# A recurrent attention with a gated layer behind it: the second sub of tokens also in fp16 pairs, and the lowest bits of a decoded weight written by ScalarE

## The chip, the core and the metric

The kernel runs on one NeuronCore of a Trainium2 chip. The metric is the device time of the core in microseconds, lower is better. Three runs of the kernel before gave 606.37, 607.78 and 608.83 us; the median is 607.78.

## What is computed

Cut to what matters:

```python
k_n = k / (norm(k) + 1e-6)                    # batch 4, 8 heads, 768 steps, 48 wide
for t in range(768):
    y[t] = q[t] @ state                       # read before the write
    v_old = k_n[t] @ state
    state = state + beta[t] * outer(k_n[t], v[t] - v_old)
x = y as 3072 tokens x 384
out = ((x @ w_a) * (x @ w_b)) @ w_out         # 384 -> 1536 -> 384
```

All of it is float32 at the interface. The weights reach the kernel as eight bytes per number (a double), and are turned into float32 on the chip.

## The kernel before, in words

**Attention.** The 768 steps are cut into 24 chunks of 32 steps, each with all 32 heads. For every chunk, TensorE makes the grams of k with k and of q with k (step G), VectorE solves a triangular system by 31 pairs of a multiplication and a subtraction (`solve`, tiles `tmp` and `b`), and then come the steps that hang on the state: K (`duo<-sh,rawb`, what the state gives), the subtraction `f`, U (`duo<-f,tt`), A (`duo<-u,at`, the output) and S (`S_ps<-u,knb`, the new state). Four chunks make a group, whose solve is one run on VectorE; `prep` makes its grams. In the first group the solve is by halves, which adds steps W and X (`bank<-b,tt`, `bank<-b,mk`, `bank<-wr,xn`). Chunks 0 and 1 run ahead of everything else.

**The gated layer.** Two chunks are a sub of 256 tokens; there are 12 subs. A sub is worked off in 12 units, one for each 128 of the 1536 inner columns (`moe`). A unit is `ab` (both products with w_a and w_b, into one PSUM bank), a copy `a` by ScalarE, the product `g` by VectorE, and two units later `moe_out`, the product with w_out that is summed over the 12 units in two banks. For the first `FULL` = 2 subs all of this is in float32: a unit is 6 matmuls of 128x256 for `ab` and 2 of 128x384 for the output, each of which the trace records twice. For the other ten, every operand is a pair of fp16 numbers, high and low part, and three of the four products are made: 18 matmuls for `ab` and 6 for the output. That asks for more on the other engines: `g` is cut into `ghl` (a cast by ScalarE, a subtraction by VectorE), a chunk's output is scaled and cut (four squares on ScalarE with `n`, a sum over partitions by TensorE, some ten short VectorE operations, `xb`), and the weights are cut into pairs.

**The weights.** `decode` makes float32 of a weight's 12 blocks, 1152 columns each, from the two words of a double: one shift (`TENSOR_SCALAR`), then two operations (`SCALAR_TENSOR_TENSOR`) that put in the sign and top bit and the lowest three bits; all three are VectorE's. Blocks lie in three staging slots (`late`, and two in `stage`), so block b + 3 is loaded only when block b is decoded; blocks 3 to 5 have places of their own in `wt`. `scales` squares each block (ScalarE, `sqw`), sums (TensorE), and when all 12 are there makes the scales: one matmul `norm,ones`, some dozen short VectorE operations from `sg` to `zw`, `gs` and `po`, then squares of w_out and a second matmul `so,ones`. `split` then writes high parts (ScalarE, `ACTIVATE wt<-wt,zw`) and low parts (VectorE, `SCALAR_TENSOR_TENSOR wt<-wt,zw` twice and `wt<-wt,eo` once a block).

**What sets the order.** Nearly every instruction is recorded by `Plan` and issued in an order that `pack` makes from a table of prices and of due times (`slot`, `when`, the `plan.due` lines); that is why the profile shows L560 for almost all. `merge`, `weave` and the calls at the end of `tile_kernel` set only the sequence in which work is recorded. Loads are chained by one-element copies on GpSimd so that few are under way at a time. Matmuls into `bank` use four PSUM banks shared by all; `duo` and `S_ps` have two each.

```python
V.tensor_scalar(d, hi, 5, 2, op0=ALU.logical_shift_left, op1=ALU.logical_shift_right)
V.scalar_tensor_tensor(d, hi, -0x40000000, d, op0=ALU.bitwise_and, op1=ALU.bitwise_or)
V.scalar_tensor_tensor(d, lo, 29, d, op0=ALU.logical_shift_right, op1=ALU.bitwise_or)
```

Of the kernel before, what the change touches and what calls it, by code (L numbers as in the profile page):

```python
# [30 lines left out]
NFC = FF // P  # L31

HALVES = [1, 0, 0, 0, 0, 0]
FULL = 2


LEADS = 4.0
BASE, FRESH, UNIT = 38e3, 4.6e3, 3.6e3


def when(v):
    n = NFC * FULL
    return BASE + (v * FRESH if v < n else n * FRESH + (v - n) * UNIT)


def finish(c):
    return 6 * c - 6 - (-2.5 if c == 4 else min(LEADS, 0.5 * max(0, c - 5)))


def slot(c, piece):  # L50
    if piece == "G" and c < 4:
        v = -30 + 0.1 * c
    elif c < 2:
        v = {
            0: {"W": -20, "X": -19, "U": -17, "A": -13.1, "S": 1.0},
            1: {"W": -15.2, "X": -14, "K": -15, "Q": -11.1, "U": -13, "A": -11, "S": 2.0},
        }[c].get(piece, -30)
    elif c < 4 and piece != "G":
        v = {
            2: {"W": 2.5, "X": 3.2, "K": 3.8, "U": 4.6, "S": 5.2, "A": 5.8},  # L60
            3: {"W": 6.2, "X": 6.8, "K": 7.4, "U": 8.2, "A": 9.0, "S": 10.4},
        }[c].get(piece, -30)
    elif piece == "G":
        v = 5.0 + 2.2 * (c - 4) if c < 8 else finish(c // 4 * 4 - 4 + c % 4 // 2) - 0.5 + 0.1 * (c % 2)
    else:
        v = finish(c) - {"W": 7, "X": 6.5, "K": 5.5, "U": 4.0, "S": 3, "A": 1.5}[piece]
    return when(v)


EARLY = [(0, "k"), (0, "b"), (2, "k"), (0, "r"), (2, "r")], [(0, "m"), (0, "v"), (2, "v"), (0, "w"), (1, "w")], [(2, "w")], [(3, "w"), (4, "w"), (4, "k"), (4, "r"), (5, "w")], [(6, "w"), (6, "k"), (6, "r"), (7, "w"), (4, "v"), (6, "v"), (8, "w")]  # L70
SHARE, QUOTA = {32: 0.24, 48: 0.19, 64: 0.5}, 1515.0
# [14 lines left out]
class Plan:  # L86
# [53 lines left out]
    def region(self, ap):  # L140
# [14 lines left out]
        p0, free = divmod(low, el)  # L155
        parts, mask = 1, (1 << (size // 2)) - 1
        for st, n in reversed([(abs(d[0]), d[1]) for d in ap.ap]):
# [171 lines left out]
    def pack(self, pri, back=False):  # L329
# [18 lines left out]
        while len(done) < n:  # L348
# [215 lines left out]
def tile_kernel(ctx, tc, kqt, kqs, kn, vn, beta, w, masks, picks, out):  # L564
# [162 lines left out]
    def scales():  # L727
        for b in range(NFC):
            v = wf[:, plain(b) : plain(b) + 6 * P]
            sq = sqr()  # L730
            plan.due = when(b + 8)
            plan.behind = set(hold)
# [15 lines left out]
            yield  # L748
        plan.due = when(15)
        t = att()  # L750
# [20 lines left out]
        V.tensor_scalar_mul(big[:, 3:4], big[:, 1:2], 2.0**-25)  # L771
        V.tensor_scalar_mul(eo, po, big[:, 2:3])
        yield

# [96 lines left out]
    def prep(g):  # L871
        chs = GROUPS[g]
        ss = sst
        for c in chs[::2]:
            kept = list(hold)
            hold.extend(opened[NFC + 1 : NFC + 2] if g == 2 else [])
            if g > 1:
# [244 lines left out]
    def steps(g, chs):  # L1122

        for c in chs:
# [290 lines left out]
    for c, what in EARLY[3]:  # L1415
        load(c, what)
    run_all(ws[3])
    queue.extend((s, list(range(NFC))) for s in range(2))
    load(0, "s")
    V.tensor_copy(sum16, sel[:, 0:P])  # L1420

    def weave(g, steps_):
# [128 lines left out]
```

## Time and profile before

| | |
|---|---|
| median of the three runs | 607.78 us |
| profiled execution, first to last instruction | 604.4 us |
| TensorE busy | 597.3 us (99%) |
| VectorE busy | 405.2 us (67%) |
| ScalarE busy | 300.6 us (50%) |
| granted TensorE clock | 1.00 in the whole span |

The profile gives the profiled execution's time as its span, and no other; the median stands 3.4 us above it, which is taken as what lies around the span. Times in the rows are counted from the start of the span. A row of the timeline has a start, a length, the engine, the line, the operation with the tile written and the tiles read, its shape and count, and in brackets how long the engine had been idle and what released it. A float32 matmul is two records, and so is a small one.

### The profile page before, as it was taken

How to read it: one execution, taken by the hardware profiler on the slowest of the kernel's cores; microseconds unless marked ns; L12 is line 12 of the kernel's file. 1: busy time of each engine (PE TensorE's matmuls, PEld its weight loads, DVE VectorE, ACT ScalarE, POOL GpSimd, SP SyncE). 2: the span in 40 equal slices, each digit the busy share in tenths (PEclk: the TensorE clock that was granted, in tenths of full speed). 3: DMA queues.
4: the chain of work that ended last, by engine and by line, in shares of the span. 5: the costliest groups of instructions: out<-in, count | busy, mean ns of one | idle time of the engine just before them, and what ended most of it. 6: DMA issues, size and time to landing. Idle time of an engine off the chain costs nothing.

```text
span 604.4 us, 25265 instructions
## 1 busy us (share of the span) xinstructions
PE 597.3 (99%) x11473; PEld 466.3 (77%) x11473; DVE 405.2 (67%) x1093; ACT 300.6 (50%) x756; POOL 34.9 (6%) x49
## 2 busy tenths in 40 slices
PE   8999999999999999999999999999999999999997
PEld 5487867777777778787878778778878878887875
DVE  5997888999799824898654996454995244244222
ACT  4321323698754664466455457545446535535332
POOL 1011320001100101000101001001000000000000
PEclk9999999999999999999999999999999999999999
DMA  5738681612212004103032021010000000000000
GB/s 207 288 123 312 243 309 36 210 71 87 73 58 98 29 29 150 38 30 124 3 89 95 3 91 61 4 54 3 3 28 4 2 28 2 3 29 2 27 1 26
DMA packets 11931, 46.46 MB, mean 77 GB/s; under 512 B 1328, under 2 KB 4784, under 8 KB 8752
## 3 DMA queue, kind: packets, MB, share of 16 engines
q1 hardware_dynamic: 11824, 44.85, 21.1%
q8 instruction: 89, 1.46, 1.0%
q14 instruction: 18, 0.15, 0.1%
HBM read 40.13 MB, written 4.72 MB: 74 GB/s over the span
## 4 chain that ended last, share of the span: by engine, by line
PE 82%; DVE 7%; DMA 5%; ACT 4%; issue 1%; POOL 0%; SPq 0%; POOLq 0%; DVEq 0%
PE bank L560 68%; PE duo L560 11%; DVE wt L560 4%; PE S_ps L560 3%; DMA rawb<-in_kqt 2%; ACT sqf L560 1%; DMA stage<-in_w 1%; DVE b L560 1%; ACT wt L560 1%; DMA late<-in_w 1%; DMA vnb<-in_vn 1%; DVE tmp L560 1%; PE bank L551 0%; ACT y L560 0%; DVE g L560 0%
## 5 line engine op out<-in xcount | busy, mean ns | idle before, releaser
L560 PE MATMUL bank<-xb,wt 128*128 128x256 f16 (+1 forms) x1800 | 246.9, 291 | 0.0
L560 PEld LDWEIGHTS <-wt 128*128 128x128 f16 x2160 | 208.2, 98 | 35.1 <-issue 0.2
L560 DVE TENSOR_TENSOR g<-bank,a 128x256 f32<-128x256 f32 x144 | 60.4, 419 | 117.2 <-ACT a L560 116.2
L560 PE MATMUL bank<-wt,ghl 128*128 128x384 f16 x720 | 136.7, 326 | 0.0
L560 ACT ACTIVATE a<-bank,gs 128x256 f32<-128x256 f32 x120 | 56.7, 472 | 125.1 <-PE bank L560 124.7
L560 PEld LDWEIGHTS <-ghl 128*128 128x128 f16 x720 | 67.5, 98 | 34.6
L560 PE MATMUL bank<-stage,wt 128*128 128x256 f16 x648 | 76.7, 273 | 0.0
L560 DVE TENSOR_TENSOR ghl<-g,ghl 128x256 f16<-128x256 f32 x120 | 51.3, 427 | 33.9 <-ACT ghl L560 33.3
L560 ACT CAST ghl<-g 128x256 f16<-128x256 f32 x120 | 48.4, 403 | 50.3 <-DVE g L560 50.1
L560 PEld LDWEIGHTS bank<-xb,wt 128*128 128x128 f32 x288 | 53.6, 190 | 10.7 <-DVE xb L560 0.5
L560 DVE TENSOR_TENSOR b<-b,tmp 128x31 f32<-128x31 f32 (+20 forms) x170 | 56.5, 332 | 3.6
L560 DVE TENSOR_TENSOR tmp<-b,b 128x31 f32<-128x31 f32 (+20 forms) x170 | 56.3, 331 | 3.6
L560 ACT COPY y<-duo 32x384 f32<-32x384 f32 x88 | 41.3, 469 | 2.1 <-PE duo L560 1.0
L560 PE MATMUL bank<-wt,g 128*128 128x384 f32 x96 | 36.9, 502 | 0.5 <-issue 0.5
L560 POOL TENSOR_TENSOR vnb<-vnb,nm 128x384 f32<-128x384 f32 x20 | 18.2, 928 | 126.3 <-DMA vnb<-in_vn 99.5
L560 ACT COPY u<-duo 128x768 f32<-128x768 f32 (+1 forms) x23 | 18.0, 784 | 11.4 <-PE duo L560 11.3
L560 PEld LDWEIGHTS bank<-wt,g 128*128 128x128 f32 x96 | 17.0, 190 | 8.1 <-issue 1.6
L560 ACT COPY a<-bank 128x256 f32<-128x256 f32 x24 | 8.8, 368 | 28.0 <-PE bank L560 28.0
L560 ACT ACTIVATE sqy<-y 128x96 f32<-128x96 f32 x80 | 22.3, 278 | 0.9
L560 DVE TENSOR_TENSOR f<-vnb,duo 128x768 f32<-128x768 f32 (+1 forms) x23 | 21.4, 929 | 1.3 <-PE duo L560 1.2
L560 PEld LDWEIGHTS duo<-f,tt 32*32 32x32 f32 x1408 | 16.4, 105 | 7.0 <-issue 3.3
L560 PEld LDWEIGHTS duo<-sh,rawb 48*64 48x64 f32 x1152 | 18.4, 135 | 4.0 <-issue 2.5
(156 smaller groups left out, 617.5 us busy)
## 6 DMA issues: line engine op xcount, KB each, us to landing
rawb<-in_kqt SPq DMA_DIRECT2D x10, 1024.0 KB, 5.1
stage<-in_w SPq DMA_DIRECT2D x6, 1152.0 KB, 7.9
vnb<-in_vn SPq DMA_DIRECT2D x12, 384.0 KB, 4.7
out<-ob SPq DMA_DIRECT2D x24, 192.0 KB, 1.9
knb<-in_kn SPq DMA_DIRECT2D x10, 384.0 KB, 3.7
stage<-in_kqs SPq DMA_DIRECT2D x8, 448.0 KB, 3.8
late<-in_w SPq DMA_DIRECT2D x3, 1152.0 KB, 6.8
wt<-in_w SPq DMA_DIRECT2D x3, 1152.0 KB, 6.6
```

The lines of the kernel that those rows point to most:

```text
L560: fn(*(self.place(a, lease) for a in args), **{k: self.place(a, lease) for k, a in kw.items()})
```

## The change

`FULL` becomes 1: the second sub of tokens (chunks 2 and 3) is also worked off in fp16 pairs, with all that belongs to it. In `decode` the third VectorE operation goes; instead ScalarE reads the top byte of each low word, makes its upper three bits of it (a scale of 1/32 and a bias, rounded on writing), and writes them over the lowest byte of the high word in the staging slot; the mask of the remaining VectorE operation takes them along. The planner's map of what is read and written learns bytes. The squares of a block are due earlier, grams of chunks 4 to 7 go into the shared banks and not into `duo`, and many due times are other numbers. Factor `big` is multiplied into `fact` of chunks 2 and 3 afterwards, since it is made later than they are. The planner gets one more rule for TensorE: where a long group would stall on the fetching of its program, a short one is taken first. One load (block 8) moves ahead of two loads of v.

```diff
-FULL = 2
+FULL = 1
-BASE, FRESH, UNIT = 38e3, 4.6e3, 3.6e3
+BASE, FRESH, UNIT = 38e3, 4781, 3604
...
-        v = 5.0 + 2.2 * (c - 4) if c < 8 else finish(c // 4 * 4 - 4 + c % 4 // 2) - 0.5 + 0.1 * (c % 2)
+        v = [2.15, 3.5, 4.5, 5.5][c - 4] if c < 8 else finish(c // 4 * 4 - 4 + c % 4 // 2) - 0.5 + 0.1 * (c % 2)
...
+                if e == "PE" and not back and can[e] and ops[i].words > 63:
+                    idle.words, idle.dur = ops[i].words + self.LOOK, ops[i].dur
+                    if self.stall(idle, t, pos, edge, come, then)[0] > self.STALL:
+                        other = [x for x in heapq.nsmallest(12, can[e]) if ops[x[1]].words < 20 and not ops[x[1]].banks - set(held)]
...
         V.tensor_scalar(d, hi, 5, 2, op0=ALU.logical_shift_left, op1=ALU.logical_shift_right)
-        V.scalar_tensor_tensor(d, hi, -0x40000000, d, op0=ALU.bitwise_and, op1=ALU.bitwise_or)
-        V.scalar_tensor_tensor(d, lo, 29, d, op0=ALU.logical_shift_right, op1=ALU.bitwise_or)
+        by = place(b).bitcast(U8).rearrange("p (a l) -> p l a", l=8)
+        A.activation(by[:, 4], by[:, 3], AF.Copy, scale=1 / 32, bias=-31 / 64)
+        V.scalar_tensor_tensor(d, hi, -0x3FFFFFF9, d, op0=ALU.bitwise_and, op1=ALU.bitwise_or)
...
-            plan.due = when(b + 8)
+            plan.due = when(b + 0.5)
             plan.behind = set(hold)
             A.activation(sq, v, AF.Square)
...
-            ga = (duo[:, ci % 2] if g or ci < 1 else att()).rearrange("p (q n) -> p q n", n=64)
+            ga = (duo[:, ci % 2] if ci < 1 and not g else att()).rearrange("p (q n) -> p q n", n=64)
...
-            V.tensor_scalar(fact[:, c : c + 1], n[:, 0:1], n[:, 0:1], big[:, 3:4], op0=ALU.mult, op1=ALU.mult)
+            if c < 2 * FULL + 2:
+                V.tensor_mul(fact[:, c : c + 1], n[:, 0:1], n[:, 0:1])
...
-    queue.extend((s, list(range(NFC))) for s in range(2))
+    queue.extend((s, list(range(NFC))) for s in range(FULL))
...
-    merge((moes, 15), (sv[1], 8))
+    merge((moes, 4), (sv[1], 8))
     while pend:
         moe_out(*pend.pop(0))
     run_all(sp)
+    queue.extend((s, list(range(NFC))) for s in range(FULL, 2))
```

How it moves instructions is shown at three places; `b_0` to `b_3` are the solve's four tiles, and numbers behind a name tell copies of a tile apart. The first is ScalarE ahead of the first unit of the gated layer, where `y_89` and `y_90` are the outputs of chunks 0 and 1, from which that unit's input is made. Before:

```order
L560 COPY wt<-duo 128x384
L560 COPY y_89<-bank_61 128x4x3x32
L560 COPY u_72<-duo 128x384
L560 COPY y_90<-bank_62 128x4x3x32
L560 ACTIVATE sqw_119<-wt 128x768
```

Now:

```order
L572 COPY wt<-duo 128x384
L572 ACTIVATE late<-late 128x1152
L572 ACTIVATE stage<-stage 128x1152 x2
L572 COPY y_89<-bank_61 128x4x3x32
L572 COPY u_72<-duo 128x384
L572 COPY y_90<-bank_62 128x4x3x32
```

Three byte operations have come ahead of the copy of chunk 0's output.

The second is VectorE where the later blocks are decoded. Before, three operations of a block stand together, ahead of the solve:

```order
L560 TENSOR_SCALAR wt<-stage 128x1152
L560 SCALAR_TENSOR_TENSOR wt<-stage,wt 128x1152 x2
L560 TENSOR_SCALAR wt<-late 128x1152
L560 SCALAR_TENSOR_TENSOR wt<-late,wt 128x1152 x2
L560 TENSOR_TENSOR g_98<-bank_62,a_96 128x256
L560 TENSOR_SCALAR wt<-stage 128x1152
```

Now:

```order
L572 TENSOR_SCALAR wt<-late 128x1152
L572 TENSOR_TENSOR g_97<-bank_64,a_95 128x256
L572 TENSOR_TENSOR b_2_69<-b_2_69,tmp 128x29x3
L572 STREAM_TRANSPOSE yt_91<-y_89 128x384
L572 TENSOR_TENSOR tmp<-b_1_68,b_2_69 128x112
L572 TENSOR_REDUCE n_0_141<-n_0_141 128x1
L572 TENSOR_TENSOR b_2_69<-b_2_69,tmp 128x28x4
L572 SCALAR_TENSOR_TENSOR wt<-late,wt 128x1152
L572 TENSOR_SCALAR wt<-stage 128x1152
```

One of the three is gone, steps of the second group's solve and of chunk 2's cut stand between the other two, and the solve has begun before the last blocks are decoded.

The third is TensorE behind the matmul that sums all blocks' squares. Before, float32 units of both subs follow it:

```order
L560 MATMUL bank_61<-norm,ones 128x24
L560 MATMUL bank_62<-xb,wt 128x256 x3
L560 MATMUL bank_64<-xb,wt 128x256 x6
L560 MATMUL bank_63<-wt,g_97 128x384
L560 MATMUL bank_61<-wt,g_97 128x384
L560 MATMUL bank_62<-xb,wt 128x256 x6
L560 MATMUL bank_63<-wt,g_98 128x384
L560 MATMUL bank_61<-wt,g_98 128x384
```

Now:

```order
L572 MATMUL bank_64<-norm,ones 128x24
L572 MATMUL bank_61<-xb,wt 128x256 x6
L572 MATMUL bank_64<-xb,wt 128x256 x6
L572 LDWEIGHTS sum_111
L572 MATMUL bank_61<-n_1_113,sum_111 128x4
L572 MATMUL bank_62<-wt,g_99 128x384
L572 MATMUL S_ps<-u_72,knb 48x48 x32
L572 MATMUL bank_63<-wt,g_99 128x384
L572 MATMUL bank_61<-xb,wt 128x256 x6
...
L572 LDWEIGHTS wt
L572 MATMUL bank_64<-xb,wt 128x256
```

Three float32 units are left behind it; the first fp16 matmul, which needs a cut weight, stands right behind these.

## Rows read from the trace of the kernel before

**Rows 1.** The page: its span, busy time by engine, and the chain's shares by line.

```profile
span 604.4 us, 25265 instructions
...
PE 597.3 (99%) x11473; PEld 466.3 (77%) x11473; DVE 405.2 (67%) x1093; ACT 300.6 (50%) x756; POOL 34.9 (6%) x49
...
PE bank L560 68%; PE duo L560 11%; DVE wt L560 4%; PE S_ps L560 3%; DMA rawb<-in_kqt 2%; ACT sqf L560 1%; DMA stage<-in_w 1%; DVE b L560 1%; ACT wt L560 1%; DMA late<-in_w 1%; DMA vnb<-in_vn 1%; DVE tmp L560 1%; PE bank L551 0%; ACT y L560 0%; DVE g L560 0%
```

**Rows 2.** Windows: stretch, its length, busy us (count) by engine, clock, DMA.

```profile
70.00:100.00 30.00, 28.93 (x670) 22.17 (x660) 24.94 (x33) 7.43 (x17) 6.80 (x10) 1.00 0.55 203
100.00:120.00 20.00, 20.00 (x252) 16.02 (x251) 18.76 (x60) 11.04 (x27) 0.36 (x1) 1.00 0.46 148
120.00:140.00 20.00, 20.00 (x264) 15.47 (x263) 18.63 (x57) 19.94 (x52) 1.01 (x2) 1.00 0.19 66
```

**Rows 3.** Timeline of PE: one float32 unit after another.

```profile
123.35 1.45 PE L560 MATMUL bank<-wt,g 128*128 128x384 f32 x4
124.64 2.75 PE L560 MATMUL bank<-xb,wt 128*128 128x256 f32 x12
127.23 1.45 PE L560 MATMUL bank<-wt,g 128*128 128x384 f32 x4
```

**Rows 4.** Timeline of PE: fp16 units, and the sum of a chunk's squares.

```profile
526.99 0.17 PE L560 MATMUL bank<-n,sum 128*128 128x4 bf16 x1
...
581.02 2.13 PE L560 MATMUL bank<-stage,wt 128*128 128x256 f16 x18
582.98 1.14 PE L560 MATMUL bank<-wt,ghl 128*128 128x384 f16 x6
583.96 2.13 PE L560 MATMUL bank<-stage,wt 128*128 128x256 f16 x18
```

**Rows 5.** Timeline of PE: first float32 unit, S, K, norms, U of chunk 4.

```profile
40.54 2.86 PE L560 MATMUL bank<-xb,wt 128*128 128x256 f32 x12
...
101.10 0.93 PE L560 MATMUL S_ps<-u,knb 32*48 32x48 f32 x64
...
112.73 1.15 PE L560 MATMUL duo<-sh,rawb 48*64 48x48 f32 x64
...
115.36 0.30 PE L560 MATMUL bank<-norm,ones 128*128 128x24 f32 x2
...
133.36 0.88 PE L560 MATMUL duo<-f,tt 32*32 32x48 f32 x64
```

**Rows 6.** Timeline of DVE: last block's shift, first scale operation, the solve's transposition.

```profile
92.19 0.77 DVE L560 TENSOR_SCALAR wt<-stage 128x1152 int32<-128x1152 int32 x1 [0.48 <-DMA stage<-in_w]
...
115.69 0.18 DVE L560 TENSOR_SCALAR sg<-bank 128x24 f32<-128x24 f32 x1
...
130.59 1.24 DVE L560 STREAM_TRANSPOSE b<-b 128x1024 f32<-128x1024 f32 x1
```

**Rows 7.** Groups of VectorE by shape: xcount, busy us, mean ns of one.

```profile
L560 DVE TENSOR_TENSOR ghl<-g,ghl 128x256 f16<-128x256 f32 x120 | 51.3, 427 | 33.9 <-ACT ghl L560 33.3
...
L560 DVE SCALAR_TENSOR_TENSOR wt<-stage,wt 128x1152 int32<-128x1152 int32 x12 | 16.7, 1391 | 0.4
...
L560 DVE SCALAR_TENSOR_TENSOR wt<-wt,zw 128x384 f16<-128x384 f32 x24 | 15.4, 642 | 2.7 <-ACT wt L560 2.7
...
L560 DVE TENSOR_REDUCE ss<-sqf 128x16 f32<-128x768 f32 x12 | 11.4, 951 | 7.4 <-ACT sqf L560 7.3
...
L560 DVE TENSOR_TENSOR b<-b,tmp 128x252 f32<-128x252 f32 x10 | 4.2, 420 | 0.2
```

**Rows 8.** Groups of ScalarE by shape.

```profile
L560 ACT CAST ghl<-g 128x256 f16<-128x256 f32 x120 | 48.4, 403 | 50.3 <-DVE g L560 50.1
...
L560 ACT COPY tt<-b 128x256 f32<-128x256 f32 x20 | 12.4, 631 | 0.9 <-DVE b L560 0.8
...
L560 ACT ACTIVATE sqw<-wt 128x768 bf16<-128x768 f32 x12 | 9.9, 847 | 1.2 <-ACT ob L560 0.6 <-PE bank L560 0.6
```

**Rows 9.** Timeline of ACT: the copy of chunk 0's output.

```profile
36.55 0.48 ACT L560 COPY y<-bank 128x384 f32<-128x384 f32 x1 [3.99 <-PE bank L560]
```

More of the change, by code (lines that the diff above doesn't have):

```diff
@@ L16 @@
 I32 = mybir.dt.int32
+U8 = mybir.dt.uint8
 BF16 = mybir.dt.bfloat16
@@ L54, in slot @@
         v = {
-            0: {"W": -20, "X": -19, "U": -17, "A": -13.1, "S": 1.0},
-            1: {"W": -15.2, "X": -14, "K": -15, "Q": -11.1, "U": -13, "A": -11, "S": 2.0},
+            0: {"W": -20, "X": -19, "U": -17, "A": -13.1, "S": 2.55},
+            1: {"W": -15.2, "X": -14, "K": -15, "Q": -11.1, "U": -13, "A": -11, "S": 0.25},
         }[c].get(piece, -30)
@@ L59, in slot @@
         v = {
-            2: {"W": 2.5, "X": 3.2, "K": 3.8, "U": 4.6, "S": 5.2, "A": 5.8},
-            3: {"W": 6.2, "X": 6.8, "K": 7.4, "U": 8.2, "A": 9.0, "S": 10.4},
+            2: {"W": 2.2, "X": 3.12, "K": 3.5, "U": 4.3, "S": 5.95, "A": 5.83},
+            3: {"W": 6.51, "X": 7.11, "K": 7.71, "U": 8.35, "A": 9.19, "S": 10.71},
         }[c].get(piece, -30)
     elif piece == "G":
-        v = 5.0 + 2.2 * (c - 4) if c < 8 else finish(c // 4 * 4 - 4 + c % 4 // 2) - 0.5 + 0.1 * (c % 2)
+        v = [2.15, 3.5, 4.5, 5.5][c - 4] if c < 8 else finish(c // 4 * 4 - 4 + c % 4 // 2) - 0.5 + 0.1 * (c % 2)
     else:
-        v = finish(c) - {"W": 7, "X": 6.5, "K": 5.5, "U": 4.0, "S": 3, "A": 1.5}[piece]
+        v = finish(c) + ([0.51, -0.7, 0.9, 1.8][c - 4] if c < 8 else 0) - {"W": 7, "X": 6.5, "K": 5.5, "U": 4.0, "S": 3, "A": 1.5}[piece]
     return when(v)
-EARLY = [(0, "k"), (0, "b"), (2, "k"), (0, "r"), (2, "r")], [(0, "m"), (0, "v"), (2, "v"), (0, "w"), (1, "w")], [(2, "w")], [(3, "w"), (4, "w"), (4, "k"), (4, "r"), (5, "w")], [(6, "w"), (6, "k"), (6, "r"), (7, "w"), (4, "v"), (6, "v"), (8, "w")]
+EARLY = [(0, "k"), (0, "b"), (2, "k"), (0, "r"), (2, "r")], [(0, "m"), (0, "v"), (2, "v"), (0, "w"), (1, "w")], [(2, "w")], [(3, "w"), (4, "w"), (4, "k"), (4, "r"), (5, "w")], [(6, "w"), (6, "k"), (6, "r"), (7, "w"), (8, "w"), (4, "v"), (6, "v")]
 SHARE, QUOTA = {32: 0.24, 48: 0.19, 64: 0.5}, 1515.0
@@ L155, in region @@
         p0, free = divmod(low, el)
-        parts, mask = 1, (1 << (size // 2)) - 1
+        parts, mask = 1, (1 << max(1, size // 2)) - 1
         for st, n in reversed([(abs(d[0]), d[1]) for d in ap.ap]):
@@ L373, in pack @@
                 i = heapq.heappop(can[e])[1]
+                if e == "PE" and not back and can[e] and ops[i].words > 63:
+                    idle.words, idle.dur = ops[i].words + self.LOOK, ops[i].dur
+                    if self.stall(idle, t, pos, edge, come, then)[0] > self.STALL:
+                        other = [x for x in heapq.nsmallest(12, can[e]) if ops[x[1]].words < 20 and not ops[x[1]].banks - set(held)]
+                        other = [x for x in other if self.stall(ops[x[1]], t, pos, edge, come, then)[0] < 50.0]
+                        if other:
+                            can[e].remove(other[0])
+                            can[e].append((pri[i], i))
+                            heapq.heapify(can[e])
+                            i = other[0][1]
                 if e == "PE" and not back and can[e] and self.stall(ops[i], t, pos, edge, come, then)[0] > self.STALL:
@@ L498 @@
     CALM = 40e3
+    LOOK = 40
     SOON = 2000.0
@@ L748, in scales @@
             yield
-        plan.due = when(15)
+        plan.due = when(NFC - 3)
         t = att()
@@ L875, in prep @@
             kept = list(hold)
-            hold.extend(opened[NFC + 1 : NFC + 2] if g == 2 else [])
+            hold.extend(opened[NFC - 2 : NFC - 1] if g == 2 else [])
             if g > 1:
@@ L1251, in steps @@
             V.tensor_reduce(n[:, 0:1], t4, AX.X, ALU.add)
-            V.tensor_scalar(fact[:, c : c + 1], n[:, 0:1], n[:, 0:1], big[:, 3:4], op0=ALU.mult, op1=ALU.mult)
+            if c < 2 * FULL + 2:
+                V.tensor_mul(fact[:, c : c + 1], n[:, 0:1], n[:, 0:1])
+            else:
+                V.tensor_scalar(fact[:, c : c + 1], n[:, 0:1], n[:, 0:1], big[:, 3:4], op0=ALU.mult, op1=ALU.mult)
             yT = ytr()
```

3 lines of the change are left out of this document (2 added, 1 removed).

## Prediction

> **What bounds the kernel now.** I read the page first [rows 1]: TensorE is busy for 597.3 of 604.4 us, and the chain that ended last runs through its matmuls into `bank` for 68% of the span. What TensorE does is the time, so a change is worth what it takes off TensorE, less what it makes TensorE wait. The windows come next [rows 2]. The reader is to see two things there. TensorE stood idle for 1.07 us between 70 and 100 us (30.00 less 28.93) and not at all from 100 to 140 us; that 1.07 us is all that a better order can give back there. And VectorE (18.76 and 18.63 of 20 us) and ScalarE (19.94 of 20 us from 120 on) have little room in just the stretch in which weights are cut into pairs. The timelines [rows 3 to 6, 9] give starts that can be subtracted, and the groups by shape [rows 7, 8] the price of one instruction.
>
> **Term 1, TensorE's own work.** A float32 unit recurs after 127.23 - 123.35 = 3.88 us: 2.59 for `ab` (127.23 - 124.64) and 1.29 for the output (124.64 - 123.35) [rows 3]. An fp16 unit recurs after 583.96 - 581.02 = 2.94 us: 1.96 and 0.98 [rows 4]. Twelve units change kind: 12 x 0.94 = 11.3 us less. Added are two sums of squares for chunks 2 and 3, at most 0.17 us each by their row and less in a stream [rows 4], which I leave out. Grams keep their number and size, only their banks are others: nothing. The scales' squares keep their number too.
>
> **Term 2, the wait for the first cut weight.** Before, sub 1 needed decoded weights only; now its first matmul needs the scales, and these need the last block. Two sums meet at the matmul `norm,ones`.
>
> TensorE's own arrival. Before, it went from the first unit (40.54) to that matmul (115.36) in 74.8 us [rows 5], 73.7 without the 1.07 idle. Counting the orders over the same stretch, 13.5 `ab` and 12 outputs stood there and now 9 and 8 do; one K (at most 1.15) and one S (0.93) [rows 5] have also gone behind it. 73.7 - 4.5 x 2.59 - 4 x 1.29 - 1.15 - 0.93 = 54.8, so TensorE would be there at 95.3 us.
>
> The data's arrival. The last block's shift began at 92.19 us, 0.48 us of which it had waited for the transfer [rows 6]. All blocks pass the same three slots and the same chain of loads as before, so I keep 92.2. Then come the shift (0.77, rows 6), the byte operation, the other VectorE operation (1.39, rows 7), the square (0.85, rows 8), and some 0.5 for the sum, the copy and hand-overs beyond, an estimate from the 0.30 us that `norm,ones` itself takes [rows 5].
>
> The byte operation is on no row. Nearest is ScalarE on contiguous data: 403 ns for 256 columns and 847 for 768 [rows 8], thus 0.87 ns a column, and 847 + 384 x 0.87 = 1.18 us for 1152. The other end is the copy `tt`, which reads with a stride of 128 bytes and takes 631 ns for 256 columns, 228 more than the cast, 0.89 ns a column [rows 8]: 1.18 + 1152 x 0.89 = 2.2 us, and 3.2 us if writing with a stride costs as much again. Below 0.85 us, what 768 columns take, nothing speaks for it, and a shorter one would gain nothing elsewhere. I take 1.18: the step here is 8 bytes, nearer to contiguous than to 128, and VectorE reads that very step in 0.77 us for 1152 columns [rows 6]. The Trainium skill says in "SBUF — State Buffer", section "Door 1: The DMA port swizzle", that a line of SBUF is 16 bytes and that full speed wants two hits in each; a step of 8 bytes has two, so by it the operation is not slowed, and no row here shows it for ScalarE.
>
> 92.2 + 0.77 + 1.18 + 1.39 + 0.85 + 0.5 = 96.9, and with four hand-overs of about 0.1 us 97.3. TensorE waits for 97.3 - 95.3 = **2.0 us**. Bounds: 0 if the slots turn over 2 us sooner since VectorE has less to do, 4 if the longer way through ScalarE delays two generations of loads by 1 us each.
>
> The first unit itself is not later: three byte operations stand ahead of the copy of chunk 0's output, 3 x 1.18 = 3.5 us, in a place where ScalarE had been idle for 3.99 us [rows 9].
>
> **Term 3, VectorE behind the scales.** It must now finish the solve of chunks 4 to 7 while it cuts weights, and U of chunk 4 waits for that solve. Before, from `sg` to the end of the solve's transposition, it took from 115.69 to 131.83 (130.59 + 1.24) [rows 6], 16.1 us. The order now has the same work there and more: 11 more solve steps (36 for 25; 0.42 each), 3 more `g` and 3 `ghl` (0.35 each: 0.43 less the 0.08 that neighbours overlap), 3 more weight parts (0.56), 2 reductions `ss` (0.87) [rows 7], the cut of chunk 3 and an `f`, four operations between 0.42 and 0.95, some 2.3, and 18 short ones at 0.09 (an estimate: half of the 0.18 of `sg` [rows 6], since short ones start in a neighbour's shadow). 4.6 + 2.1 + 1.7 + 1.7 + 2.3 + 1.6 = 14.0; 16.1 + 14.0 = 30.1 us. It starts at about 97.7 and ends at 127.8; ScalarE's copy `tt` (0.63, rows 8) and two hand-overs bring 128.7.
>
> TensorE from `norm,ones` to that U: 3 float32 `ab` and 4 outputs (7.8 + 5.2), S, K and two tiny matmuls (0.9 + 1.1 + 0.3), 5.5 fp16 `ab` and 2 outputs (10.8 + 2.0): 28.1 us, thus 125.4 us. The same count for the order before (4.5 `ab`, 4.5 outputs) gives 17.8 us, and 133.36 - 115.36 is 18.0 [rows 5], so the count holds. Wait: 128.7 - 125.4 = **3.3 us**, between 0 (VectorE's extra work half hidden) and 8 (each part waits for ScalarE too).
>
> Behind that U the weights' last parts have time: VectorE needs some 24 us more for them, and TensorE's order holds about 27 us of work ahead of the last unit that wants one. The operations of the decode that leave VectorE (12 x 1.39 = 16.7 us) are worth nothing by themselves, since TensorE doesn't wait for VectorE there; they make room for the grams and the solve that were drawn forward. That cover gone, the solve would start late and Term 3 grow by as much.
>
> **Sum.** -11.3 + 2.0 + 3.3 - 1.07 (the old idle, which these waits replace) = -7.1; I take -7 us. Against the profiled execution's 604.4 us that is 597.4; against the median, 3.4 above, **600.8 us**. By the bounds of the two waits alone it is 595.4 (neither) to 607.4 (4 and 8 us).
>
> **The rivals.**
>
> *Full cover.* Both waits vanish, because VectorE and the loads run ahead once a third of the decode has left VectorE. For it: VectorE had idle time between 70 and 100 us, 30.00 - 24.94 [rows 2]. Against it: TensorE now has little else to do until the scales are there. -11.3 - 1.07 = -12.4 at most; some wait will stay: 596.5.
>
> *VectorE and ScalarE bound each other.* Every low part waits for its high part, and both engines were full in this stretch already [rows 2]. If the 30 us become 35, U comes at 133.4, as late as before, and Term 3 is 8: -11.3 + 2.0 + 8.0 - 1.07 = -2.4, 605.4.
>
> *The byte operation pays for its stride at one side* (2.2 us). Three of them ahead of chunk 0's copy overrun the idle time: 6.6 - 3.99 = 2.6 us. The last block comes two generations of slots and two byte operations later, about 4 us. The larger decides, perhaps with more behind it: -7 + 4 to -7 + 7, about 606.
>
> *It pays at both sides* (3.2 us); this is the case that ends slower. Place: ScalarE between 44 and 97 us, where nine of these operations stand among squares and copies `a` that units wait for, all in one queue. Price: between 4 and 9 times the excess over 1.18 us, as more of the nine lie on the path; at an excess of 2.0 us that is 8 to 18 us, or 608.8 to 618.8, and I put it at 613. With a factor of 7 the point at which the gain is gone is an excess of 1 us, an operation of 2.2 us, and slower by over 0.5% begins at 2.6 us. The Trainium skill's "ScalarE: Activation LUTs", section "Rules for kernel authors", speaks against the change here: plain arithmetic belongs on VectorE, by its estimate up to three times faster an element. Rows 7 and 8 don't bear that out for this form: VectorE takes 1391 ns for its 1152 columns, ScalarE by its slope 1180. By the rule the case would be likelier than I make it.
>
> **Chances.** The forecast 0.60, full cover 0.10, the two engines bound 0.10, one side 0.10, both sides 0.10. A measurement here tells some 0.5% from no change, 3.0 us. Of the forecast nearly all lies more than that below 607.8, full cover wholly, of the next two a part: faster 0.73. Within 3.0 us lie most of these two: 0.15. Slower 0.12, nearly all of the last. The range runs from full cover, 596.5, to the middle of the one-sided stride, 606.5; it leaves out the both-sided case and half of the one-sided.
>
> **What would show it.** Right: fp16 units with 2.94 us between them from about 110 us on; `ACTIVATE stage<-stage` at about 1.18 us; `norm,ones` at about 97 us; U of chunk 4 near 129 us, released by ScalarE's `tt`, with TensorE idle some 2 and 3 us ahead of the two; TensorE busy about 586 us. Wrong: a byte operation over 2 us, the first unit later than 41 us, or TensorE idle before many of sub 1's units.

## The result and the profile after

The changed kernel takes 615.87 us (median of four runs, 615.02 to 616.16); the kernel before, on the same chip, 607.14. The ratio is 1.0136, its interval 1.0107 to 1.0164: slower by 8.7 us, where 7 us faster was forecast and 596.5 to 606.5 given as the range.

The page first, to be held against [rows 1]: the span, the engines, and the chain's shares by engine.

```profile
span 613.2 us, 25514 instructions
...
PE 590.1 (96%) x11571; PEld 458.9 (75%) x11571; DVE 396.2 (65%) x1116; ACT 340.2 (55%) x798; POOL 35.0 (6%) x49
...
PE 72%; DVE 14%; ACT 11%; issue 1%; DMA 1%; POOL 0%; SPq 0%; ACTq 0%
```

TensorE is busy for 7.2 us less than before, and the span is 8.8 us longer: its idle time went from 7.1 to 23.1 us (613.2 less 590.1). The windows say where it went; columns as in [rows 2].

```profile
70.00:100.00 30.00, 22.98 (x580) 17.17 (x580) 19.90 (x49) 19.51 (x33) 7.04 (x9) 0.89 0.57 200
100.00:120.00 20.00, 17.88 (x309) 13.09 (x310) 16.89 (x52) 15.74 (x32) 1.57 (x2) 1.00 0.49 150
120.00:140.00 20.00, 20.00 (x229) 15.97 (x219) 19.92 (x68) 18.91 (x50) 0.00 (x0) 1.00 0.26 87
...
88.00:94.00 6.00, 4.59 (x28) 3.62 (x25) 6.00 (x18) 0.90 (x2) 1.20 (x1) 0.50 0.27 80
```

From 70 to 100 us TensorE is busy for 22.98 of 30 us, with VectorE at 19.90 and ScalarE at 19.51: no engine is full. That is the picture of a chain that goes back and forth between engines, not of one engine that bounds. The groups of ScalarE by shape name the link; these rows answer to the shapes of [rows 8].

```profile
L572 ACT ACTIVATE stage<-stage 128x1152 uint8<-128x1152 uint8 x6 | 16.6, 2804 | 2.4 <-POOL stage L572 2.1 <-DVE wt L572 0.3
L572 ACT ACTIVATE late<-late 128x1152 uint8<-128x1152 uint8 x3 | 8.4, 2791 | 0.0
```

The byte operation takes 2.79 us; the prediction had taken 1.18. What that does ahead of the first unit stands in ScalarE's timeline, against [rows 9]; its last row is the byte operation of the last block.

```profile
31.90 2.80 ACT L572 ACTIVATE late<-late 128x1152 uint8<-128x1152 uint8 x1
34.44 5.43 ACT L572 ACTIVATE stage<-stage 128x1152 uint8<-128x1152 uint8 x2
39.59 0.61 ACT L572 COPY y<-bank 128x384 f32<-128x384 f32 x1
...
106.78 2.79 ACT L572 ACTIVATE stage<-stage 128x1152 uint8<-128x1152 uint8 x1 [0.28 <-DVE wt L572]
```

The copy `y` had waited for TensorE and come at 36.55; now it queues behind three byte operations until 39.59. VectorE's timeline has the other side of the last block, against [rows 6]: its shift begins at 105.95 and not at 92.19, and the operation behind it has waited 1.42 us for ScalarE.

```profile
105.95 0.75 DVE L572 TENSOR_SCALAR wt<-stage 128x1152 int32<-128x1152 int32 x1
...
109.60 1.36 DVE L572 SCALAR_TENSOR_TENSOR wt<-stage,wt 128x1152 int32<-128x1152 int32 x1 [1.42 <-ACT stage L572]
```

How often VectorE waits like that is told by its waits between 28 and 112 us: who waited for what, us in all, times, longest.

```profile
DVE wt L572 <- ACT wt L572: 8.8, 3, 3.0
DVE wt L572 <- ACT stage L572: 6.3, 4, 2.9
...
DVE wt L572 <- ACT norm L572: 3.2, 2, 1.9
DVE wt L572 <- DMA wt<-in_w: 2.8, 1, 2.8
DVE wt L572 <- ACT s L572: 1.7, 1, 1.7
...
DVE wt L572 <- ACT late L572: 0.9, 1, 0.9
```

The rows with `wt` and ACT are VectorE's waits ahead of its second operation on a block, and they last until the byte operation ends. (Those put down to `norm` and `s` end there too: one at 98.78, where the byte operation had begun at 95.97 and takes 2.78.) They make 20.9 us, in 11 of the 12 blocks. The only wait for a load is one of 2.8 us, at block 3.

TensorE's marks, against [rows 5]: the first unit, an `ab` at half clock, `norm,ones`, the first fp16 unit, and U of chunk 4.

```profile
42.94 1.56 PE L572 MATMUL bank<-xb,wt 128*128 128x256 f32 x6
...
90.07 4.80 PE L572 MATMUL bank<-xb,wt 128*128 128x256 f32 x12
...
112.94 0.40 PE L572 MATMUL bank<-norm,ones 128*128 128x24 f32 x2
...
126.30 1.92 PE L572 MATMUL bank<-xb,wt 128*128 128x256 f16 x16
...
142.98 0.88 PE L572 MATMUL duo<-f,tt 32*32 32x48 f32 x64 [0.59 <-ACT tt L572]
```

The forecast had these at 40.54, 97.3, about 110 and 128.7. The first is 2.4 us late, `norm,ones` 15.6, U of chunk 4 14.3: once the scales are there, the lateness stays what it is. A part is the clock. TensorE, with little to do from 84 on, ran at 0.50 of its 2.4 GHz between 88 and 94 us, and an `ab` of twelve took 4.80 us there for the 2.75 of [rows 3]: 2.05 us.

### The profile page after: what moved, and what is told of

Its sections match the earlier page's. It is cut to its first block, busy times and chain, and to the rows that moved or that the text cites. A ratio compares the mean times of both kernels' runs of the same rounds, so it can differ in the third digit from the quotient of the medians.

```text
span 613.2 us, 25514 instructions
## 1 busy us (share of the span) xinstructions
PE 590.1 (96%) x11571; PEld 458.9 (75%) x11571; DVE 396.2 (65%) x1116; ACT 340.2 (55%) x798; POOL 35.0 (6%) x49
## 4 chain that ended last, share of the span: by engine, by line
PE 72%; DVE 14%; ACT 11%; issue 1%; DMA 1%; POOL 0%; SPq 0%; ACTq 0%
PE bank L572 58%; PE duo L572 9%; DVE wt L572 4%; DVE b L572 3%; PE S_ps L572 3%; ACT stage L572 2%; ACT wt L572 2%; DVE tmp L572 2%; PE bank L563 2%; DVE g L572 1%; ACT y L572 1%; ACT late L572 1%; DVE ss L572 1%; DMA knb<-in_kn 1%; DVE ghl L572 1%
## 5 line engine op out<-in xcount | busy, mean ns | idle before, releaser
L572 PEld LDWEIGHTS <-wt 128*128 128x128 f16 x2376 | 229.1, 98 | 39.7 <-issue 1.1
L572 PE MATMUL bank<-xb,wt 128*128 128x256 f16 (+1 forms) x1872 | 241.8, 283 | 1.1 <-ACT norm L572 1.1
L572 PE MATMUL bank<-wt,ghl 128*128 128x384 f16 x792 | 151.7, 326 | 0.4 <-DVE wt L572 0.4
L572 ACT ACTIVATE a<-bank,gs 128x256 f32<-128x256 f32 x132 | 62.4, 473 | 139.3 <-PE bank L572 138.8
L572 PEld LDWEIGHTS <-ghl 128*128 128x128 f16 x792 | 73.8, 98 | 39.4 <-issue 1.6
L572 DVE TENSOR_TENSOR ghl<-g,ghl 128x256 f16<-128x256 f32 x132 | 56.8, 431 | 34.4 <-ACT ghl L572 33.8
L572 DVE TENSOR_TENSOR tmp<-b,b 128x31 f32<-128x31 f32 (+20 forms) x170 | 56.2, 331 | 3.1
L572 PEld LDWEIGHTS bank<-xb,wt 128*128 128x128 f32 x144 | 27.9, 200 | 9.3 <-ACT norm L572 1.7
L572 PE MATMUL duo<-sh,rawb 48*64 48x48 f32 x1152 | 21.4, 223 | 0.5 <-issue 0.3
L572 ACT COPY sh<-S_ps 112x768 f32<-112x768 f32 x22 | 17.6, 798 | 7.6 <-PE S_ps L572 7.5
L572 PE MATMUL bank<-wt,g 128*128 128x384 f32 x48 | 19.0, 509 | 1.6 <-ACT wr L572 1.6
```

The source lines that it names most:

```text
L572: fn(*(self.place(a, lease) for a in args), **{k: self.place(a, lease) for k, a in kw.items()})
```

## The experiments

Theory **P**: the byte operation's price, 2.79 us on the path of every block, is the whole loss; the rest of the forecast holds. Its rivals: **N**, sub 1 needs the scales so early that TensorE must wait whatever the decode does; **O**, the planner, which reckons such an operation at about 1.05 us, made an order for the wrong price; **H**, a step through ScalarE costs by its hand-overs and its place in the queue, however short it is.

**1. The third part of the bits by VectorE again**, all else as changed.

```diff
-        by = place(b).bitcast(U8).rearrange("p (a l) -> p l a", l=8)
-        A.activation(by[:, 4], by[:, 3], AF.Copy, scale=1 / 32, bias=-31 / 64)
-        V.scalar_tensor_tensor(d, hi, -0x3FFFFFF9, d, op0=ALU.bitwise_and, op1=ALU.bitwise_or)
+        V.scalar_tensor_tensor(d, hi, -0x40000000, d, op0=ALU.bitwise_and, op1=ALU.bitwise_or)
+        V.scalar_tensor_tensor(d, lo, 29, d, op0=ALU.logical_shift_right, op1=ALU.bitwise_or)
```

> The changed kernel with the decode of before: VectorE puts in the lowest three bits with its second SCALAR_TENSOR_TENSOR, ScalarE has no byte operation; FULL stays 1 and all due times stay. Theory P (the price of the byte operation, 2.79 us in the trace where 1.18 were taken, makes the loss: it delays the first unit, and through ScalarE's queue and the three staging slots the matmul of the norms from 97 to 113 us): this gives 600 to 606 us, the norms at about 100 us, with the 12 x 1.39 us back on VectorE. Theory N (the second sub in fp16 pairs needs the scales so early that TensorE waits whoever makes the bits): 612 us or more, the norms still beyond 108 us. Theory H (it is the hand-over VectorE to ScalarE and back within a decode that costs, not the length of the operation): as P.

609.94 us, ratio 1.0066 (1.0042 to 1.0091): between what P and N had said, with `norm,ones` at 100.92, where P had it. Putting 16.7 us of work back on VectorE is 5.9 us better than ScalarE's byte operation, and still slower than before. Its windows:

```profile
70.00:100.00 30.00, 25.67 (x611) 19.13 (x611) 27.60 (x49) 8.46 (x25) 7.27 (x10) 0.94 0.55 194
...
120.00:140.00 20.00, 17.05 (x225) 12.61 (x228) 19.96 (x61) 13.05 (x28) 3.70 (x3) 1.00 0.06 22
169.00:200.00 31.00, 27.58 (x493) 21.89 (x486) 30.00 (x101) 13.02 (x34) 0.00 (x0) 1.00 0.08 25
```

Here one engine comes near to bounding: where TensorE lacks most (4.3, 3.0 and 3.4 us), VectorE is busy for 27.60 of 30, 19.96 of 20 and 30.00 of 31 us. The relief of VectorE was needed; what was wrong is the price paid for it.

**2. The operation left out**: the same edit as in 1 without its last line, so that the lowest three bits of a weight stay zero.

> The changed kernel without the byte operation and with nothing in its place: the lowest three bits of every decoded weight are left zero, so a part of the decode is not computed. VectorE keeps its relief, ScalarE has nothing more. Theory P: this is what the forecast was made for, less the byte operation altogether, 597 to 602 us, the norms at about 95 to 98 us. Theory N: 610 us or more. Theory H: as P.

601.14 us, ratio 0.9919 (0.9895 to 0.9943): 14.7 us less than the changed kernel (13 by the two ratios), by twelve operations of 2.79 us. Its page, and TensorE's marks:

```profile
span 597.5 us, 25495 instructions
...
PE 585.8 (98%) x11571; PEld 457.4 (77%) x11571; DVE 394.2 (66%) x1116; ACT 309.5 (52%) x786; POOL 33.8 (6%) x49
```

```profile
40.80 1.56 PE L572 MATMUL bank<-xb,wt 128*128 128x256 f32 x6 [0.17 <-DVE xb L572]
...
96.95 0.40 PE L572 MATMUL bank<-norm,ones 128*128 128x24 f32 x2
...
110.09 2.13 PE L572 MATMUL bank<-xb,wt 128*128 128x256 f16 x18
...
129.19 0.88 PE L572 MATMUL duo<-f,tt 32*32 32x48 f32 x64 [0.87 <-ACT tt L572]
```

TensorE is busy for 585.8 us (forecast: about 586) and idle for 11.7; the marks stand at 40.80, 96.95, 110.09 and 129.19. Against the changed kernel's profile (590.1 and 23.1), 11.4 of the 15.7 us of span are idle time and 4.3 are the same matmuls taking longer, the low clock among the reasons. N falls: TensorE lacks no more than 1.82 us between 70 and 100, and none of that directly ahead of `norm,ones`. It is these three waits:

```profile
79.69 2.86 PE L572 MATMUL bank<-xb,wt 128*128 128x256 f32 x12 [0.22 <-ACT norm L572]
...
83.81 0.29 PE L572 MATMUL bank<-wide,sqw 128*128 128x1 bf16 x6 [1.13 <-ACT norm L572]
...
84.56 0.29 PE L572 MATMUL bank<-wide,sqw 128*128 128x1 bf16 x6 [0.47 <-DVE g L572]
```

**3. The kernel before with the byte operation** in its decode, nothing else of the change.

> The kernel before with the byte operation in its decode and nothing else of the change: both first subs in float32. Theory P: the same delays of the first unit (2 to 3 us) and of the blocks (two generations of slots and two operations) stand here too, though sub 1 needs no scales early: 611 to 618 us. Theory N: the byte operation alone does little, 606 to 609 us. Theory H: between the two, 608 to 612 us, since three hand-overs of some 0.2 us come to each of 12 blocks.

616.5 us, ratio 1.0154 (1.0118 to 1.0189). The operation alone costs that kernel 10.4 us, though it takes 16.7 us of work off VectorE; H had said 612 at most. TensorE's work is that of before (597.7 us); the first unit starts at 43.36, `norm,ones` at 121.74 for 115.36.

**4. The price by itself**: behind the work of the kernel before stand operations of 1152 columns, one after another, each with another pattern.

```diff
+    for out_, in_ in (
+        (se[:, :, 4], se[:, :, 3]),
+        (db[:, 0:1152], sb[:, 0:1152]),
+        (db[:, 0:1152], se[:, :, 3]),
+        (de[:, :, 4], sb[:, 0:1152]),
+        (dw[:, :, 1], sw[:, :, 0]),
+        (dst.bitcast(F32)[:, 0:1152], src.bitcast(F32)[:, 0:1152]),
...
+        A.activation(out_, in_, AF.Copy, scale=1 / 32, bias=0.0)
...
+    V.tensor_scalar(de[:, :, 4], se[:, :, 3], 5, None, op0=ALU.logical_shift_right)
...
+    G.tensor_scalar(de[:, :, 4], se[:, :, 3], 1 / 32, -31 / 64, op0=ALU.mult, op1=ALU.add)
```

> The kernel before with eight operations behind its last output, one after another, that only have a price: on ScalarE 1152 columns as the change does them (bytes at a step of 8, in place), bytes to bytes without a step, bytes read at a step of 8 and written without, bytes read without a step and written at 8, float32 read and written at a step of 8 bytes, float32 without a step; then on VectorE a shift of bytes at a step of 8 on both sides, and on GpSimd the scale and bias on the same bytes. If the step is what costs at both sides: 2.8, 1.2, 2.0, 2.0, 2.8, 1.2 us. If writing with a step costs all: 2.8, 1.2, 1.2, 2.8, 2.8, 1.2. If bytes are slow on ScalarE whatever their step: 2.8, 2.8, 2.8, 2.8, 1.2, 1.2. VectorE 0.8 (if it goes at the rate of the decode's shift) or 1.3 us; GpSimd 1 to 4 us. The time of the whole has no meaning.

Timeline in the order of the list: bytes read and written at a step of 8 bytes; bytes contiguous at both sides; bytes read at that step and written contiguously; the reverse; float32 words at a step of 8 bytes at both sides; float32 words contiguous; then VectorE and GpSimd with bytes at that step at both sides.

```profile
600.25 2.74 ACT L561 ACTIVATE late<-late 128x1152 uint8<-128x1152 uint8 x1
603.01 1.16 ACT L561 ACTIVATE stage<-late 128x1152 uint8<-128x1152 uint8 x1
604.21 1.21 ACT L561 ACTIVATE stage<-late 128x1152 uint8<-128x1152 uint8 x1
605.46 2.75 ACT L561 ACTIVATE stage<-late 128x1152 uint8<-128x1152 uint8 x1
608.24 1.21 ACT L561 ACTIVATE stage<-late 128x1152 f32<-128x1152 f32 x1
609.48 1.16 ACT L561 ACTIVATE stage<-late 128x1152 f32<-128x1152 f32 x1
...
610.67 1.44 DVE L561 TENSOR_SCALAR stage<-late 128x1152 uint8<-128x1152 uint8 x1 [11.95 <-ACT stage L561]
...
612.28 2.73 POOL L561 TENSOR_SCALAR stage<-late 128x1152 uint8<-128x1152 uint8 x1 [203.93 <-issue]
```

Reading bytes with the step costs next to nothing (1.21 for 1.16), and so does writing whole words with it (1.21 for 1.16). Writing bytes with it makes 1.16 into 2.75. On ScalarE the step as such is not the price, and the cost is not shared between the sides: it is the stepped write of a part of a word.

**5. Two bytes for one**: ScalarE writes the lower half of the word as a uint16 (`half[:, 2]` for `by[:, 4]`).

> The changed kernel, with the one difference that ScalarE writes two bytes (a uint16) over the lower half of the high word instead of one byte over its lowest; the VectorE operation that follows masks the rest away, so nothing else moves. The price run showed that ScalarE takes 2.74 us for 1152 bytes written at a step of 8, 2.75 when they are read without a step, 1.21 when only the reading has the step, and 1.21 for float32 written at the same step: what costs is writing less than a word with a step. Theory P: if two bytes go as four do (1.2 us), the kernel becomes what was forecast, 599 to 603 us, the norms at about 97 us and the first unit at 41 us. If two bytes cost as one does (2.7 us): 614 to 617 us, as the changed kernel. Theory H (hand-overs): about 615 us in either case.

616.16 us, ratio 1.0143 (1.0095 to 1.0191), and the same duration to 2 ns:

```profile
L573 ACT ACTIVATE stage<-stage 128x1152 uint16<-128x1152 uint8 x6 | 16.5, 2802 | 2.4 <-POOL stage L573 2.1 <-DVE wt L573 0.3
```

**6. The planner told the true price**: one line in its table of costs, 2700 ns for an output of bytes.

> The changed kernel with the planner told the true price of the byte operation, 2.7 us in place of 1.05; the order of every engine is planned anew, the operation stays as slow as it is. Theory P: the loss is the operation's length on the way of the blocks, which no order takes away: 611 to 616 us, the norms beyond 108 us. Rival theory O (the loss is an order made for a price that isn't true): 600 to 606 us.

614.76 us, ratio 1.0121 (1.0071 to 1.0172), where P had said 611 to 616. `norm,ones` comes at 104.31, 8.6 us sooner than in the changed kernel and sooner than P had it (beyond 108), but the first fp16 unit only at 129.38 (there 126.30), and the time is 1.1 us less. From 70 to 100 us TensorE is busy for 22.68 of 30 us, as little as in the changed kernel, and its granted clock is 0.89, 0.88 and 0.83 in the windows from 40, 70 and 100 us on. O falls as it was put, at 600 to 606 us: this order puts the scales first and pays for the twelve operations elsewhere. A part of O stays open: TensorE is idle for 18.0 us here against 23.1, and the same matmuls take 595.1 us against 590.1, so what the new order saved in waits came back as longer matmuls, with the low clock of these windows among the reasons.

**7. The byte operation on GpSimd**, with the same scale and bias, reckoned at 2700 ns.

> The changed kernel with the byte operation on GpSimd (scale and bias as ScalarE's, 2.73 us by the price run), planned with that price. Each decode is as long as in the changed kernel, but ScalarE's queue is free of twelve operations of 2.8 us. If the length of a decode, by two generations of slots, makes the loss: 610 to 616 us. If it is ScalarE's queue, in which copies that units and norms need stand behind byte operations: 601 to 606 us. The first three operations stand in GpSimd's idle time, so the first unit should come at 41 to 42 us.

618.17 us, ratio 1.0172 (1.0123 to 1.0222), at 3.03 to 3.12 us each in the mean of a group:

```profile
L572 POOL TENSOR_SCALAR stage<-stage 128x1152 uint8<-128x1152 uint8 x6 | 18.3, 3056 | 6.9 <-DVE wt L572 6.7
```

ScalarE keeps only its own work, and neither case had a time as long (first unit at 46.43, `norm,ones` at 119.88). So taking the load off ScalarE's queue is not enough. That the link of 3 us in each block's chain is all of it isn't shown here, because two more things differ. The granted clock was 0.50 from 32 to 44 us, ahead of the first unit, and TensorE's same matmuls took 597.8 us. And VectorE was slower beside GpSimd: two shifts that take 1.42 us in the changed kernel took 3.98 here.

**8. Whole words.** Since full words cost nothing extra, ScalarE writes the byte's upper bits as an int32 over the whole low word, and VectorE merges in two long operations:

```diff
+        A.activation(lo, by[:, 3], AF.Copy, scale=1 / 32, bias=-31 / 64)
+        V.scalar_tensor_tensor(d, hi, 3, lo, op0=ALU.logical_shift_left, op1=ALU.bitwise_or)
+        V.scalar_tensor_tensor(d, hi, 0x3FFFFFFF, d, op0=ALU.bitwise_or, op1=ALU.bitwise_and)
```

> The changed kernel, but with no narrow write. ScalarE takes the same byte of the low word and writes it as a whole int32 word over that low word; VectorE then needs two of its long operations a block: (high word shifted left by 3) or that word, and then the top two bits put right by an and with the high word, whose other bits are set (this holds for weights below 2 in size, which these are). VectorE's work for a block is 2 x 1.39 = 2.78 us, against 3.55 before and in the experiment with the bits by VectorE, and 2.16 in the change. Theory P (only the price of a narrow write broke the forecast; a ScalarE operation of about 1.2 us is covered, as the prediction reckoned): ScalarE's operation takes 1.2 us, the first unit starts by 41 us, and the time lies between the two experiments without a narrow write by VectorE's share: 609.9 less 8.8 x 9.2 / 16.7 = 4.8 us, 605.1; with a longer path for the last block (1.21 + 2.78 for 0.77 + 1.39) about 606. That is level with the kernel before or 1 us faster. Theory H (any step through ScalarE costs, by the hand-overs and its queue, whatever its length): 609 to 613, norms later than 101 us, and the first unit later than 42 us.

609.77 us, ratio 1.0034 (1.0003 to 1.0065). ScalarE's operation takes 1.27 us, as P had it; but the time, the first unit at 45.76 and `norm,ones` at 105.88 are all as H had said. In the profiled run the granted clock was 0.50 from 30 to 42 us, ahead of the first unit, which neither theory had reckoned with. By itself this run decides nothing between P and H.

**9 and 10. The narrow write for blocks 0 to 2 alone, and for blocks 3 to 11 alone**; the others as in experiment 1 (`if b in BYTES:` around the two forms).

> The changed kernel with the narrow write by ScalarE for blocks 0 to 2 alone, those ahead of the first unit; blocks 3 to 11 by VectorE. To be read against the experiment with all bits by VectorE (609.9 us, first unit 40.7). If the delay of the first unit is lost and nothing gets it back: first unit about 43 us and 612 us. If the three operations cost nothing more than their place, and VectorE's 4.2 us less of work is worth its share (2.2 us): about 610. If they delay every generation of the slots behind them: 614 or more.

> The changed kernel with the narrow write by ScalarE for blocks 3 to 11 alone; blocks 0 to 2 by VectorE. The first unit starts at about 40.7 us as in the experiment with all bits by VectorE. If the loss of 14.7 us against the kernel without the bits is mostly made by the nine on the blocks' path (the place that the last rival names), the norms' matmul stands at about 110 us and the time is about 613.5 (615.9 less the 2.4 us of the first unit). If the first three make most of the loss, below 608.

The first three: 612.74 us, ratio 1.0090 (1.0061 to 1.0118), 2.8 us over experiment 1. That doesn't price them: the two intervals overlap, the clock was low ahead of the first unit here too, and in the profiles TensorE is idle as long as in experiment 1 (18.7 and 18.9 us), while its matmuls take 595.5 us for 589.5. The last nine: 614.7 us, ratio 1.0113 (1.0066 to 1.0161), within 1.2 us of the changed kernel. Their first unit is in time, and the loss is all behind it:

```profile
40.50 1.56 PE L573 MATMUL bank<-xb,wt 128*128 128x256 f32 x6 [0.39 <-DVE xb L573]
...
112.90 0.30 PE L573 MATMUL bank<-norm,ones 128*128 128x24 f32 x2
```

So the place that the last rival named, ScalarE between the first unit and the last block, holds most of the loss. VectorE's waits for it between 28 and 112 us make 18.8 us (6.7, 5.1, 4.2 and 2.8). A part is the clock here too, 0.50 from 84 to 94 us.

**11. The narrow write for blocks 6 to 8 alone**, its price known to the planner.

> The changed kernel with the narrow write by ScalarE for blocks 6 to 8 alone, the planner told its price (2.7 us); the other nine by VectorE. VectorE has 4.2 us less to do than in the experiment with all bits by VectorE (609.9 us). If ScalarE has room for three such operations there, 609.9 - 8.8 x 4.2 / 16.7 = 607.7 us, about the kernel before. If each lies on the path of the blocks with its excess, factor 1 gives 609.9 + 3 x 1.6 - 2.2 = 612.5; factor 4 as over all of them, 617 or more.

607.24 us, ratio 0.9991 (0.9958 to 1.0025): level with the kernel before, as the first case had it. Three such operations find room; nine, planned at the old price in experiment 10, did not.

**12. Whole words for blocks 3 to 11**, blocks 0 to 2 by VectorE.

> The experiment with whole words by ScalarE, but for blocks 3 to 11 alone; blocks 0 to 2, ahead of the first unit, by VectorE as in the kernel before. In the experiment before it the first unit started at 45.7 us and TensorE's granted clock stood at 0.50 between 30 and 42 us, so its 609.8 us tells little of ScalarE's share. Here the first unit should start at about 41 us with the clock at 1.00 ahead of it. Theory P (a ScalarE operation of 1.27 us is covered): VectorE has 9 x 0.77 = 6.9 us less to do than in the experiment with all bits by VectorE, and 609.9 - 8.8 x 6.9 / 16.7 = 606.3 us, the norms at 99 to 101 us. Theory H (a step through ScalarE costs whatever its length): the nine lie on the path of the blocks as in the experiment with nine narrow writes, the norms stand later than 104 us, and the time is 609 or more.

607.22 us, ratio 0.9990 (0.9958 to 1.0023). The time is P's (606.3), but the first unit is late, and `norm,ones` stands at 104.67, later than 104 as H had said. The windows show why (the columns as before, the clock third from the end), and TensorE's timeline what it does to a single group: the matmul `duo<-wt` below took 1.14 us in experiment 1.

```profile
30.00:40.00 10.00, 10.00 (x198) 8.29 (x200) 5.29 (x7) 0.76 (x2) 0.00 (x0) 0.50 0.02 3
```

```profile
34.45 1.95 PE L572 MATMUL duo<-wt 64*64 64x48 f32 x32
...
45.53 1.54 PE L572 MATMUL bank<-xb,wt 128*128 128x256 f32 x6
...
104.67 0.30 PE L572 MATMUL bank<-norm,ones 128*128 128x24 f32 x2
```

What ScalarE's step costs the blocks is therefore read between these marks, behind the slow stretch. From the first unit to `norm,ones` it is 59.1 us here, 60.1 in experiment 8 (105.88 - 45.76), 60.2 with VectorE alone (100.92 - 40.69), 56.2 without the bits, but 70.0 in the changed kernel and 72.4 with the nine narrow writes, some of these last two being the clock. Against VectorE alone, a step through ScalarE of 1.27 us lengthens that stretch by nothing, and one of 2.79 by some 10 us. VectorE's waits say the same without TensorE's marks: between 28 and 112 us it waits for ScalarE ahead of its operations on the blocks for 3.1 us here, against 18.8 with nine narrow writes.

```profile
DVE wt L572 <- ACT wt L572: 2.5, 2, 1.7
...
DVE wt L572 <- ACT stage L572: 0.6, 2, 0.3
```

And the time is below that of experiment 1, the two intervals apart. H falls.

No kernel here that decodes all bits beats the one before. The change's other parts, with the relief of VectorE and no bits made, are worth 5.0 us (experiment 2: 606.14 less 601.14), and experiments 11 and 12 keep none of it that a measurement can tell. What the clock takes of that is open: in experiment 12's profile TensorE is idle for 12.9 us, nearly as little as in experiment 2, but its matmuls take 595.0 us for 585.8; its two executions with a granted clock of 1.000 took 604.04 and 605.47 us, where eight executions of the kernel before at that clock took 604.66 to 608.18.

## Why the prediction was wrong

**The step that failed** is the price of the byte operation, "I take 1.18". The bounds were 0.85 and 3.2 us, and the truth of 2.79 lay inside; the choice between them, "nearer to contiguous than to 128", was wrong. VectorE reading that step in 0.77 us [rows 6] is a row about reading words; experiment 4 agrees with it for ScalarE's reading of bytes (1.21 us), but what costs here is writing. No row of before showed a narrow stepped write, so none could bear the choice.

The Trainium skill's "SBUF — State Buffer", section "Door 1: The DMA port swizzle", by which two hits in a line of 16 bytes are enough for full speed, fits the stepped reads and the stepped words of experiment 4 and not its stepped byte writes: same step, same lines, 2.75 us for 1.21. The measurement decides; the rule as it stands does not cover them.

**What hung on it.** "The first unit itself is not later": 3 x 2.79 = 8.4 us into 3.99 of idle time; the unit came 2.4 us late. Term 2: the byte operation in the last block's sum is 1.6 us longer, but the larger part is "All blocks pass the same three slots and the same chain of loads as before, so I keep 92.2". With the price wrong the shift stood at 105.95, 13.8 us later; in experiment 2 it begins at 91.82. The path that the prediction had for a delay, slots and loads ("two generations of loads by 1 us each"), is not the one that the trace shows: behind block 3 no shift waited for a load. What waited was VectorE, in the fixed order of its own work, for the byte operation of nearly every block. Three waits come from blocks 3 to 5, which use no slot; this one is block 3's:

```profile
51.49 1.36 DVE L572 SCALAR_TENSOR_TENSOR wt<-wt 128x1152 int32<-128x1152 int32 x1 [3.05 <-ACT wt L572]
```

**What held.** Experiment 2 is the forecast with the price at nothing instead of 1.18. Term 1: TensorE busy 585.8 us for 586. Term 2: `norm,ones` at 96.95 for 97.3 (without the operation the sum gives 96.1; the shift came 0.4 us sooner and what stands behind it took 1.2 us longer than reckoned). Its wait has the right size by luck: TensorE's 1.82 us lie between 79 and 85 us, at earlier blocks, and from 85 to 97 it was busy for the whole 12 us, since the order found it other work. Term 3: U of chunk 4 at 129.19 for 128.7, released by `tt`; but its wait was 0.87 us and not 3.3, because TensorE had more work ahead of it than the count of the order gave, and another 1.34 us of idle time came from 140 to 169. Idle in all: 11.7 us, where the prediction's terms make 7.1 - 1.07 + 2.0 + 3.3 = 11.3. So its 601.14 us, against the forecast's 600.8, comes out of Term 1 as reckoned and out of waits whose sum is right and whose places are not, and it does less work than the change. Of the 3.4 us that were added for what lies around the span, about half is the spread between executions: the changed kernel's profiled execution took 615.02 us for its 613.2.

**The relief of VectorE.** "Worth nothing by themselves" was too low: between experiments 1 and 2 the 16.7 us are worth 8.8. The sentence behind it, that Term 3 grows by as much when the cover is gone, was too high, and experiment 1 shows the loss at several places rather than at one.

**The rivals.** The one that came is "pays at both sides", 613 us at a chance of 0.10. Its place was right (experiment 10). Its mechanism was half right: one side pays, and all of it; and what stood waiting was VectorE before its second operation, more than "copies `a` that units wait for" (between 42 and 110 us `g` waits 4.9 us for `a`, and 7.1 in experiment 2). Its price was a little low: with an excess of 1.61 us over 1.18, the distance from 600.8 to 615.9 is a factor of 9.4, above the 4 to 9 given. Its rule from the Trainium skill, "ScalarE: Activation LUTs", section "Rules for kernel authors", spoke against the change rightly for this form, though the page gives its factor of up to about three for bf16 alone: VectorE does the same byte shift in 1.44 us, ScalarE's takes 2.74. For whole words no run bears it out: ScalarE's 1.27 us is less than VectorE's 1.39 for one operation. The chance of 0.10 was too small for an operation whose form no row showed, with a loss that starts at 2.2 us in a bracket reaching 3.2.

## What to carry to other kernels

An operation of a new form (another element size, another step on the writing side) has no price until it has run: put the forms behind the end of a running kernel and read five durations in one trace, before a plan is built on one of them. When a step on another engine is put between two operations of an engine that works in a fixed order, its price can count at every block and not once at the end: here VectorE waited 20.9 us for twelve such steps, and an excess of 1.6 us an operation became 13 to 15 us. And where ScalarE is to write a part of a word with a step, try the whole word: 1.27 us for 2.79, though here no kernel came out ahead by it.

## What the runs showed of the hardware

A write of one or two bytes with a step of 8 bytes took ScalarE 2.74 to 2.80 us for 1152 columns, a write of four bytes with that step 1.21, and GpSimd wrote such bytes in 2.73 us alone and 3.03 to 3.12 in the mean beside other work. VectorE wrote them in 1.44. While GpSimd wrote them, two of VectorE's shifts took 3.98 us instead of 1.42.

TensorE's granted clock fell to 0.50 (1.2 GHz) in several places. In the changed kernel it stood there from 88 us on, behind a stretch with TensorE busy for 2.29 of 4 us. In experiment 11 it fell at 34 us, behind a stretch with 2.68 of 4. In experiments 8, 9 and 12 it fell near 29 us, though TensorE was busy for 9.76, 9.61 and 9.50 of the 10 us from 20 to 30; in experiment 1 the clock stayed at 1.00 there with 9.64 of 10. These rows don't say what sets them apart, and it wasn't tried further. In experiment 12, whose first three blocks are decoded as in experiment 1, the first unit came 4.8 us later (45.53 for 40.69), more than any difference left between the times of experiments 8, 11 and 12.
